# A planned start stage: finer steps, columns in other banks, and more work inside the plan

## Chip, core and metric

One core of one Trainium2 chip runs the program. The metric is device time in microseconds from launch to end; the kernel's inputs lie in HBM at the start and its output must lie there at the end.

## What is computed

Three layers, one behind the other: block-causal attention, a feed-forward layer with a maximum over three products, and a layer with eight experts of which each token takes two.

```python
def _attn_ref(q, k, v):                  # (4, 8, 576, 64) each
    scores = scale * np.matmul(q, k.transpose(0, 1, 3, 2))
    mask = block_i >= block_j            # blocks of 64 positions
    scores = np.where(mask, scores, -1000000000.0)
    ...                                  # softmax over the last axis
    return np.matmul(attn, v)

def _moe_ref(x, w1, w2, w3, w_out):      # x: (2304, 512), d_ff = 768
    h = np.maximum(np.maximum(x @ w1, x @ w2), x @ w3)
    return h @ w_out

def _moe2_ref(x, w_gate, w_noise, noise, w1, w2):
    noisy_logits = x @ w_gate + np.log1p(np.exp(x @ w_noise)) * noise
    ...                                  # top 2 of 8 experts, softmax over the two
    out[mask] += top2_w[mask, k, None] * (np.maximum(x[mask] @ w1[e], 0.0) @ w2[e])
```

Everything is fp32. Large products are made of three products of split operands (high and low part, fp32r); the first token unit and the early attention pairs use plain fp32 products, which the trace shows as two records each (0.43 us for 256 columns, from the hidden products).

## The kernel before

**Work.** Attention runs in 32 jobs, each a pair of heads of one batch; an "early" job (e) takes the first 256 queries, a "late" one (l) the other 320. The second layer runs in nine units of 256 tokens (`UT`). Unit 0 is computed in the start stage from early jobs 0 to 3 (batch 0), unit 2 from jobs 4 to 7 (batch 1). Behind the start stage a loop over jobs 8 to 31 sets steps of a job's attention beside steps of the units that are ready (`filler`, `gap`; one hidden step counts as 2.6 us in the code's own costs). Then the experts run one after the other.

**Start stage.** `start` (L598) lists steps with an engine, a cost, dependencies and a bank kind; `Plan.run` (L63) plays them through a list schedule and emits them in the order of their planned times, under `tc.manual_schedule()`, so each engine runs its steps in that order. A ready step with the longest chain behind it goes first (`level`). Where TensorE has no ready step before the first hidden product, a warming product on a spare bank is put in (`idle`, L603; `warm`, L132).

The steps: `first_load` brings queries (as two diagonal blocks, so that one product of 128 rows serves both heads; the rest of the tile is zeroed by `new_set`, L198), keys and values of jobs 0 to 3 over the SP and ACT queues. A job then goes through `e_scores` (L313, two steps h = 0, 1 of two blocks each), `e_max` on DVE, `e_exp` on ACT, `e_sums`, `e_scale` (on DVE for jobs 1, 2, 3, else on ACT), `e_turn` (transposes), `e_copy`, `e_values` (L429) and `e_out`. The weights w1, w2, w3 and w_out arrive as the 64-bit words of double floats, in 24 pieces (`load_piece`, twelve buffers); a piece is turned into fp32 by `integers` on DVE, `low_bits` on ACT and `join` on POOL. `first_hidden` (L554) computes the 18 half steps of unit 0's hidden layer, `first_max` the maxima, `first_columns` (L573) the product with w_out and with w_out times the gates (`gate_turn`, `gate_copy`, `gate_product`, `gate_out`, three groups). `split` makes the high and low halves of the weights for the other units (ACT and POOL). Banks: two "s", four "t"; the column products take a "t" bank.

**Behind the plan**, in program order but free for the scheduler to move, even ahead of the plan's end: `init_route`, `init_ids`, unit 0's route, the loads of job 8 (`load_scores`, `load_rest`) and of the first late job 9 (`load_job`, `load_values`), zeroing for it (`late_tiles`, L218), its split into halves (`prep_job`, L260), and job 8's scores. The loop over jobs 8 to 31 follows; while job 8 is transposed, job 9's five score blocks run (`s_block`).

## Time and profile before

| | us |
|---|---|
| median of three timed runs | 999.83 |
| lowest, highest | 998.15, 1004.65 |
| the profiled execution | 998.79 |
| its span, first to last instruction | 997.0 |

The profile page gives busy time by engine and in 40 slices of some 25 us; the granted clock is that of TensorE, in tenths of 2.4 GHz. Timelines list instructions in order of time, equal neighbours merged. A number in brackets behind a row is idle time of the engine just before it, and what ended it.

### The profile page before, as it was taken

The page shows a single profiled execution, that of the slowest core. Times are in us where ns is not written, and L with a number is a line of the kernel's source. Part 1 is how long each engine was busy: PE and PEld are TensorE (multiplying, and loading weights), DVE is VectorE, ACT ScalarE, POOL GpSimd, SP SyncE. Part 2 cuts the span into 40 slices and gives each one's busy share as a digit, 9 for nine tenths or more (in the row PEclk, how much of TensorE's full clock was granted, in tenths as well). Part 3 has the DMA queues.
Part 4 walks back from the last instruction along what each step waited for, and adds up shares of the span by engine and source line. Part 5 has one row for each costly group of instructions (what it writes and reads, how often), then busy time and mean ns, then how long its engine had stood idle before and what let it go on. Part 6 is the DMA issues. An engine that isn't in the chain of part 4 may idle for free. (4 is left out here: it accounts for less than half of the span.)

```text
span 997.0 us, 17056 instructions
## 1 busy us (share of the span) xinstructions
PE 975.0 (98%) x6558; PEld 872.7 (88%) x6558; DVE 429.1 (43%) x1260; ACT 396.8 (40%) x934; POOL 393.1 (39%) x303
## 2 busy tenths in 40 slices
PE   8979998999999999999999999999999999999997
PEld 5867897999999899899999899898898979898895
DVE  7872556664667566733157332221322222221321
ACT  6686345654545545541124143232322414132210
POOL 2875120130302213111320478664746556574302
PEclk9998999999999999999999999999999999999999
DMA  8931216121112111203013366553444344342101
GB/s 260 318 109 53 100 44 203 52 59 59 33 49 70 55 54 53 83 25 99 11 37 135 115 191 188 167 189 95 142 136 155 134 140 156 117 160 84 60 12 58
DMA packets 75860, 106.15 MB, mean 106 GB/s; under 512 B 23548, under 2 KB 48124, under 8 KB 75776
## 3 DMA queue, kind: packets, MB, share of 16 engines
q1 hardware_dynamic: 63408, 75.97, 24.5%
q0 software_dynamic: 10192, 28.28, 8.7%
q8 instruction: 52, 0.85, 0.4%
q10 hardware_dynamic: 2176, 0.79, 0.3%
q14 instruction: 32, 0.26, 0.1%
HBM read 85.35 MB, written 20.53 MB: 106 GB/s over the span
## 5 line engine op out<-in xcount | busy, mean ns | idle before, releaser
L173 POOL TENSOR_TENSOR w<-rw,w 128x1536 fp32r<-128x1536 f32 (+1 forms) x42 | 131.7, 3138 | 70.6 <-ACT w L172 55.1
L752 POOL TENSOR_TENSOR hl<-hm,hh 128x512 fp32r<-128x512 f32 x21 | 27.3, 1302 | 174.8 <-ACT hh L751 174.6
L172 ACT ACTIVATE w<-rw 128x1536 fp32r<-128x1536 f32 (+1 forms) x42 | 56.5, 1345 | 86.6 <-issue 42.1
L1108 PE MATMUL b<-xh,w 128*128 128x384 f32 (+7 forms) x272 | 87.3, 322 | 0.3 <-DVE xB L1113 0.3
L1110 PE MATMUL b<-xh,w 128*128 128x384 f32 (+7 forms) x272 | 87.6, 322 | 0.0
L1109 PE MATMUL b<-xl,w 128*128 128x384 f32 (+7 forms) x272 | 87.4, 321 | 0.0
L736 PE MATMUL t<-xA,w 128*128 128x256 f32 x288 | 82.8, 287 | 0.0
L737 PE MATMUL t<-xA,w 128*128 128x256 f32 x288 | 81.8, 284 | 0.0
L738 PE MATMUL t<-xA,w 128*128 128x256 f32 x288 | 81.5, 283 | 0.0
L265 POOL TENSOR_TENSOR Kl<-rk,Kh 128x576 fp32r<-128x576 f32 x16 | 23.0, 1436 | 122.6 <-ACT Kh L264 122.6
L1113 DVE SCALAR_TENSOR_TENSOR ht<-b,ht 128x384 fp32r<-128x384 f32 (+6 forms) x56 | 29.1, 520 | 94.5 <-ACT ht L1112 94.5
L1164 POOL DMA_INDIRECT out_rows<-y,isc x37 | 37.4, 1011 | 78.1 <-DVE y L1161 73.9
L1109 PE MATMUL t<-xl,w 128*128 128x256 f32 x240 | 67.3, 281 | 0.0
L1110 PE MATMUL t<-xh,w 128*128 128x256 f32 x240 | 67.3, 280 | 0.0
L1108 PE MATMUL t<-xh,w 128*128 128x256 f32 x240 | 67.3, 281 | 0.0
L1156 PE MATMUL b<-w,ht 128*128 128x512 f32 (+1 forms) x168 | 67.0, 399 | 0.0
L1158 PE MATMUL b<-w,ht 128*128 128x512 f32 (+1 forms) x168 | 66.4, 395 | 0.0
L1157 PE MATMUL b<-w,ht 128*128 128x512 f32 (+1 forms) x168 | 66.3, 394 | 0.0
L925 POOL DMA_INDIRECT ids<-rows,slots x36 | 35.7, 991 | 72.5 <-DVE slots L922 64.3
L736 PE MATMUL t<-xB,w 128*128 128x256 f32 x216 | 61.8, 286 | 0.0
L737 PE MATMUL t<-xB,w 128*128 128x256 f32 x216 | 61.2, 283 | 0.0
L738 PE MATMUL t<-xB,w 128*128 128x256 f32 x216 | 61.1, 283 | 0.0
(396 smaller groups left out, 2784.2 us busy)
## 6 DMA issues: line engine op xcount, KB each, us to landing
rw<-in_e SPq DMA_DIRECT2D x32, 768.0 KB, 4.6
w<-in_w SPq DMA_DIRECT2D x18, 512.0 KB, 8.0
rw<-in_e SPq DMA_DIRECT2D x16, 512.0 KB, 3.7
rk<-in_kT SPq DMA_DIRECT2D x16, 288.0 KB, 3.1
x2d<-x SPq DMA_DIRECT2D x18, 256.0 KB, 2.0
out_rows<-x SPq DMA_DIRECT2D x9, 512.0 KB, 3.1
w<-in_w_out SPq DMA_DIRECT2D x6, 512.0 KB, 7.6
rq<-in_qT SPq DMA_DIRECT2D x16, 160.0 KB, 2.6
```

The lines of the kernel that those rows point to most:

```text
L172: nc.scalar.activation(t[:, 0, :c], r[:, :c], AF.Copy)
L173: nc.gpsimd.tensor_sub(t[:, 1, :c], r[:, :c], plain(t[:, 0, :c]))
L736: nc.tensor.matmul(ps[:, j], wh, x[:, 0], start=kt == 0, stop=False)
L737: nc.tensor.matmul(ps[:, j], wh, x[:, 1], start=False, stop=False)
L738: nc.tensor.matmul(ps[:, j], wl, x[:, 0], start=False, stop=kt == 3)
L1108: nc.tensor.matmul(p, wt1(e, 0, kt, f), th[:, kt, c0:c1], start=kt == 0, stop=False)
L1109: nc.tensor.matmul(p, wt1(e, 0, kt, f), tl[:, kt, c0:c1], start=False, stop=False)
L1110: nc.tensor.matmul(p, wt1(e, 1, kt, f), th[:, kt, c0:c1], start=False, stop=kt == 3)
L1156: nc.tensor.matmul(ps, a, wt2(e, 0, f), start=f == 0, stop=False)
L1157: nc.tensor.matmul(ps, a, wt2(e, 1, f), start=False, stop=False)
L1158: nc.tensor.matmul(ps, l, wt2(e, 0, f), start=False, stop=f == 7)
L1164: st = nc.gpsimd.indirect_dma_start(out=out, out_offset=bass.IndirectOffsetOnAxis(ap=at, axis=0), in_=y, in_offset=None, bounds_check=NTOK ...
```

## The change

`Plan` gets ranks (lower goes first; `level` only breaks ties), a shared transfer model (`load`), banks that come free in the order in which they were taken, and no delay between steps of one engine. Costs are changed throughout. Queries of jobs 0 to 7 are loaded in one transfer as they lie, and `e_scores` makes two products of 64 rows (one per head, each to its half of the partitions) out of one of 128; job 8 and later ones keep the diagonal form. Column products become single steps and go to the bank that served as DVE's scratch (`shifted`) and to that of the warming products; gate and logit products take the gates as the stationary operand (16 columns) and stream 256 columns, and are copied and transposed back. Warming products may be put in until the second tile's first column product. The late pair's loads, zeroing and split, job 8's loads, scores and scaling and the noise load become steps of the plan; `init_route` and `init_ids` stand ahead of it, and a scheduling barrier without a semaphore behind it, so nothing that follows is moved ahead of the plan's end. The two row stores move behind the barrier, and one `gap(8)` more is put ahead of the loop. The core of the diff:

```diff
-
...
+    def add(self, engine, cost, emit, deps=(), rank=0.0, take=None, give=None, late=0.2, load=0.0):
...
+        def can(i, t):
+            x = self.ops[i][4]
+            if x and len(taken[x]) >= self.banks[x] and given.get(taken[x][-self.banks[x]], 1e9) > t:
+                return False
+            return all((own if self.ops[d][0] == self.ops[i][0] else done).get(d, 1e9) <= t for d in self.ops[i][3])
+
         while wait:
...
+                    taken[take].append(i)
...
-                t = min([x for x in [*free.values(), *done.values(), *(g[0] for g in gives)] if x > t])
+                t = min([x for x in [*free.values(), *done.values(), *given.values()] if x > t])
         for _, emit in out:
             emit()
         return max(done.values())
...
     def new_set(q, kv, p, pt):
-        q = q.rearrange("p (i c) -> p i c", c=128)
-        for r in range(2):
-            nc.gpsimd.memset(q[64 * r:64 * r + 64, :, 64 - 64 * r:128 - 64 * r], 0.0)
...
+    def late_queries(n):
+        QQ.append(att.tile([128, 5, 128], F32R, name=("Qh", "Ql")[n]))
+        nc.gpsimd.memset(plain(QQ[n]), 0.0)
+
+    def late_tails():
         for i in (4, 6, 8):
             nc.gpsimd.memset(PL[i][:, 64 * i + 64:], 0.0)
+
+    def clear_diagonal():
+        for r in range(2):
+            nc.gpsimd.memset(diagonal(SET[0][0])[64 * r:64 * r + 64, :, 64 - 64 * r:128 - 64 * r], 0.0)
...
+    def load_queries(j, eng):
+        eng.dma_start(early_set(j)[0][:, :256], qT[at(j):at(j) + 2, :, :256].rearrange("h d n -> (h d) n"))
+
+    def load_keys(j, eng):
+        eng.dma_start(early_set(j)[1], kT[at(j):at(j) + 2, :, :256].rearrange("h d n -> (h d) n"))
...
+        q = diagonal(SET[0][0])
         for r in range(2):
             nc.sync.dma_start(q[64 * r:64 * r + 64, :, 64 * r:64 * r + 64],
-                              qT[i + r, :, 0:256].rearrange("d (n c) -> d n c", c=64))
-        nc.sync.dma_start(k, kT[i:i + 2, :, :256].rearrange("h d n -> (h d) n"))
-
...
+        load_keys(j, nc.sync)
+
...
+            n = 64 * i + 64
+            if j >= 8:
+                nc.tensor.matmul(ps[:, x:x + n], diagonal(q)[:, i], k[:, :n], start=True, stop=True)
+                continue
+            for m in (slice(0, 64), slice(64, 128)):
+                nc.tensor.matmul(ps[m, x:x + n], q[m, 64 * i:64 * i + 64], k[m, :n], start=True, stop=True)
...
-    def gate_product(g):
-        ps = GS[g] = bank()
+    def gate_product(g, k):
+        ps = GS[g] = GS[g] if k else bank()
+        nc.tensor.matmul(ps[:2 * E, :256], GT[:, k], PL[7 + k // 2][:, 256 * (k % 2):256 * (k % 2) + 256],
+                         start=k == 0, stop=k == 3)
...
+    def logit_rows(key):
+        nc.scalar.activation(PL[6][:2 * E, :256], GS[key][:2 * E, :256], AF.Copy)
+
+    def logit_turn(key):
+        ps = GS[key] = bank()
         for j in range(2):
-            for k in range(4):
-                o = 256 * (k % 2) + 128 * j
-                nc.tensor.matmul(ps[:, 2 * E * j:2 * E * j + 2 * E], PL[7 + k // 2][:, o:o + 128], GT[:, k],
-                                 start=k == 0, stop=k == 3)
-
...
-    def first_columns(tt, w, n):
-        ps = C0["p"] = bank()
-        for ft in range(6):
-            nc.tensor.matmul(ps[:, :n], M0[ft // 2][:, ft % 2, tt * 128:tt * 128 + 128], w[ft], start=ft == 0,
-                             stop=ft == 5)
+    def first_columns(tt, ft):
+        if ft == 0:
+            C0["p", tt] = spare_bank if tt else shifted.bitcast(F32)
+        nc.tensor.matmul(C0["p", tt], M0[ft // 2][:, ft % 2, tt * 128:tt * 128 + 128], WPO[ft], start=ft == 0, stop=ft == 5)
...
+        def conv(n, rank):
+            LD[n] = add("SP", 0.45, lambda: load_piece(n), [AD[n - NW]] if n >= NW else [], rank, late=2.0, load=1.3)
...
+        def work(n, rank):
+            a = add("DVE", 1.45, lambda: integers(n), [LD[n]], rank, late=0.05)
+            b = add("ACT", 0.56, lambda: low_bits(n), [LD[n]], rank)
+            AD[n] = add("POOL", 1.0, lambda: join(n), [a, b], rank, late=0.1)
...
-            p = 30.0 + 0.1 * j
             if old is None:
-                LQ[j] = add("SP", 1.25, lambda: first_load(j, nc.sync, 0), [], 0.1 * j, late=2.0)
-                LV[j] = add("ACT", 1.25, lambda: first_load(j, nc.scalar, 1), [], 0.1 * j, late=2.0)
+                one, two = (nc.sync, nc.scalar) if j % 2 == 0 else (nc.scalar, nc.sync)
+                a, b = ("SP", "ACT") if j % 2 == 0 else ("ACT", "SP")
+                LQ[j] = [add(a, 0.65, lambda: load_queries(j, one), late=2.0, load=0.4),
+                         add(b, 0.65, lambda: load_keys(j, two), late=2.0, load=0.4)]
+                LV[j] = add(a, 0.65, lambda: load_rest(j, one), late=2.0, load=0.5)
                 return
-            LQ[j] = add("SP", 1.9, lambda: load_scores(j), [ES[old, 1]], p, late=2.0)
-            LV[j] = add("SP", 0.65, lambda: load_rest(j), [EV[old]], p, late=2.0)
+            LQ[j] = [add("SP", 0.45, lambda: load_queries(j, nc.sync), [ES[old, 1]], 1.0, late=2.0, load=0.4),
+                     add("SP", 0.45, lambda: load_keys(j, nc.sync), [ES[old, 1]], 1.0, late=2.0, load=0.4)]
+            LV[j] = add("SP", 0.45, lambda: load_rest(j), [EV[old]], 1.0, late=2.0, load=0.5)
...
             sb = "t" if j in (1, 3) else "s"
+            k = 2.5 if j > 3 else 0.0
...
-                s = ES[j, h] = add("PE", (0.76, 0.34)[h], lambda h=h: e_scores(j, h, sb), [LQ[j], LV[j]], p, take=sb)
-                m = add("DVE", (0.7, 0.45)[h], lambda h=h: e_max(j, h), [s], p)
-                ex.append(add("ACT", (0.9, 0.7)[h], lambda h=h: e_exp(j, h), [m] + ([ET[old]] if old is not None else []),
-                              p, give=None if h else sb))
-            r = add("DVE", 0.2, lambda: e_sums(j), ex, p, give=sb)
...
             sc = "DVE" if j in (1, 2, 3) else "ACT"
-            c = add(sc, 1.1 if sc == "DVE" else 1.35, lambda: e_scale(j, sc), [r], p)
+            c = add(sc, 1.3, lambda: e_scale(j, sc), [r], k, late=0.15)
...
+            if j < 4:
+                EX[j] = add("ACT", 0.3, lambda: e_out(j), [v], k, give=v)
+            else:
+                x = add("ACT", 0.35, lambda: e_out(j, 0), [v], k)
+                EX[j] = add("DVE", 0.4, lambda: e_out(j, 1), [x], k, give=v)
...
-                a = add("PE", 1.73, lambda fp=fp, m=m: first_hidden(fp, m, 0), d + hid[-1:], 100.0, take="t")
-                b = add("PE", 1.73, lambda fp=fp, m=m: first_hidden(fp, m, 1), [a], 99.0)
+                a = add("PE", 1.73, lambda fp=fp, m=m: first_hidden(fp, m, 0), d + hid[-1:], 1.0, take="t")
+                b = add("PE", 1.73, lambda fp=fp, m=m: first_hidden(fp, m, 1), [a], 1.0)
                 hid.append(b)
...
-            a = add("ACT", 0.41 * cost, lambda: split(n, i, j, src, False), deps, prio)
...
+        def part(n, i, j, src, deps, cost):
+            a = add("ACT", 0.41 * cost, lambda: split(n, i, j, src, False), deps, 4.0)
+            return add("POOL", cost, lambda: split(n, i, j, src, True), [a], 4.0, late=0.1)
...
-            done_g = add("PE", 1.7, lambda g=g: gate_product(g), cs + [gt], 60.0, take="t")
...
+            a = p = add("PE", 0.43, lambda g=g: gate_product(g, 0), cs[:1] + [gt], 2.5, take="t")
+            for k in (1, 2, 3):
+                p = add("PE", 0.43, lambda g=g, k=k: gate_product(g, k), [p, cs[k // 2]], 2.5)
+            b = add("ACT", 0.33, lambda g=g: logit_rows(g), [p], 0.5, give=a)
+            c = add("PE", 0.22, lambda g=g: logit_turn(g), [b], 0.5, take="t")
+            done_g = add("DVE", 0.15, lambda g=g: logit_out(g, WPG[:, 2 * g:2 * g + 2]), [c], 0.5, give=c, late=0.1)
...
-            a = add("PE", 5.2, lambda tt=tt: first_columns(tt, WPO, DM), [last, prev] + [AD[n] for n in range(18, 24)], 100.0, take="t")
-            last = add("ACT", 0.75, lambda tt=tt: first_out(tt), [a], 24.0, give="t")
-            add("SP", 0.7, lambda tt=tt: store(0, tt, C0[tt]), [last], 24.0)
-            a = add("PE", 1.3, lambda tt=tt: first_columns(tt, [WPG[:, ft] for ft in range(6)], 2 * E), [last] + go, 100.0, take="t")
-            last = add("DVE", 0.2, lambda tt=tt: first_gates(tt), [a], 24.0, give="t")
...
+            for ft in range(6):
+                p = add("PE", 0.86, lambda tt=tt, ft=ft: first_columns(tt, ft),
+                        [prev, *(AD[n] for n in (range(24) if ft == 0 else ()))] + ([p] if ft else []), 4.0)
+                if ft == 0:
+                    until = p
+            add("ACT", 0.46, lambda tt=tt: first_out(tt), [p], 0.5)
...
+        z = add("POOL", 0.66, clear_diagonal, [ES[7, 0], ES[7, 1]], 2.5)
+        q8 = add("SP", 2.1, lambda: load_scores(8), [z], 2.5, late=2.0, load=0.8)
+        x = add("SP", 0.9, lambda: load_job(first), [LD[23], gt], 3.0, late=2.0, load=1.5)
+        add("SP", 1.0, lambda: nc.sync.dma_start(noise_sb, noise.rearrange("(t p) e -> p t e", p=128)), [x, q8], 5.0, late=2.0, load=5.0)
+        v8 = add("SP", 0.45, lambda: load_rest(8), [EV[7]], 4.0, late=2.0, load=0.5)
+        add("SP", 0.45, lambda: load_values(first), [EV[6]], 4.0, late=2.0, load=0.8)
+        add("POOL", 0.45, late_tails, [], 4.0)
+        late_q = [add("POOL", 0.65, lambda n=n: late_queries(n), [ES[4 + n, 0], ES[4 + n, 1]], 3.0) for n in (0, 1)]
+        a = add("ACT", 0.68, lambda: split_keys(first, False), [x, EV[4]], 3.0)
+        add("POOL", 1.4, lambda: split_keys(first, True), [a, EV[5]], 3.0)
+        for r in (0, 1):
+            a = add("ACT", 0.47, lambda r=r: split_queries(first, r, False), [x, late_q[0]], 3.0)
+            add("DVE", 0.5, lambda r=r: split_queries(first, r, True), [a, late_q[1]], 3.0)
+        ex = []
+        for h in (0, 1):
+            a = add("PE", (0.76, 0.44)[h], lambda h=h: e_scores(8, h), [q8], 2.5, take="s")
+            b = add("DVE", (0.94, 0.67)[h], lambda h=h: e_max(8, h), [a], 2.5, late=0.15)
+            ex.append(add("ACT", (0.86, 0.64)[h], lambda h=h: e_exp(8, h), [b, ET[7]], 2.5, give=None if h else a, late=0.1))
+        b = add("DVE", 0.29, lambda: e_sums(8), ex, 2.5, give=a, late=0.1)
+        add("ACT", 1.3, lambda: e_scale(8, "ACT"), [b], 2.5)
+        return pl, idle, until
...
-        nc.sync.dma_start(noise_sb, noise.rearrange("(t p) e -> p t e", p=128))
...
-        nc.sync.dma_start(ids.rearrange("(p c) t -> p c t", p=128), z)
+        nc.gpsimd.dma_start(ids.rearrange("(p c) t -> p c t", p=128), z)
...
+    init_route()
+    init_ids()
     pl, idle, first_product = start()
     with tc.manual_schedule():
         pl.run(idle, first_product)
+    tc.no_sync_barrier()
     ph0.close()
+    for tt in range(2):
+        store(0, tt, C0[tt])
...
-    init_route()
-    init_ids()
...
-    load_scores(EJ[0])
-    load_rest(EJ[0])
-    late_tiles()
-    load_job(first)
-    load_values(first)
-    prep_job(first)
+    RAW.pop(first)
     load_job(late_after(first))
     load_values(late_after(first))
-    for f in score_steps(8):
-        f()
     scored(8)
+    gap(8)
```

## Rows read from the trace of the kernel before

**Rows 1.** Page, parts 1 and 2: PE over the span; granted clock in 40 slices.
```profile
PE 975.0 (98%) x6558; PEld 872.7 (88%) x6558; DVE 429.1 (43%) x1260; ACT 396.8 (40%) x934; POOL 393.1 (39%) x303
...
PEclk9998999999999999999999999999999999999999
```

**Rows 2.** Busy time by stretch: length; busy and count per engine; clock; DMA share; GB/s.
```profile
0.00:26.04 26.04, 22.49 (x129) 13.53 (x129) 18.94 (x71) 16.20 (x54) 7.43 (x26) 1.00 0.86 260
26.04:45.95 19.91, 19.37 (x90) 16.66 (x89) 18.64 (x28) 13.02 (x22) 15.68 (x16) 1.00 0.97 315
45.95:68.78 22.83, 20.54 (x114) 17.87 (x115) 16.66 (x43) 16.28 (x49) 20.43 (x20) 1.00 0.45 160
68.78:86.30 17.52, 14.33 (x100) 12.13 (x99) 7.27 (x24) 15.77 (x49) 5.20 (x4) 0.81 0.32 83
86.30:108.24 21.94, 20.94 (x84) 12.98 (x83) 5.25 (x15) 8.29 (x20) 13.02 (x12) 0.84 0.08 28
108.24:400.00 291.76, 287.42 (x2291) 264.54 (x2291) 180.11 (x590) 153.94 (x413) 58.34 (x48) 1.00 0.24 70
400.00:997.00 597.00, 589.95 (x3761) 534.96 (x3756) 182.27 (x496) 173.32 (x330) 272.98 (x181) 1.00 0.35 112
```

**Rows 3.** Waits of PE behind 108 us: total, times, longest.
```profile
PE t L426 <- ACT xB L455: 2.5, 1, 2.5
```

**Rows 4.** Busy time by stretch of the warming products (L135) alone.
```profile
0.00:26.04 26.04, 11.10 (x40) 4.08 (x40) 1.00 0.86 260
```

**Rows 5.** Timeline of ACT and its queue, start stage: start, duration, engine, line, operation.
```profile
1.51 0.62 ACTq L594 DMA_DIRECT2D kve<-in_v  x1
...
7.59 1.28 ACT L653 ACT_TABLE_LOAD   x1 [7.59 <-DMA Kl<-in_v]
8.88 0.47 ACT L329 ACTIVATE pe<-s,st 128x256 f32<-128x256 f32 x1
```

**Rows 6.** Timeline of SP's queue.
```profile
15.31 8.53 SPq L251 DMA_DIRECT2D rq<-in_qT  x1
```

**Rows 7.** Timeline of PE, 0 to 86 us (fp32 products show two records each).
```profile
5.13 1.44 PE L317 MATMUL s<-kve,qe 128*128 128x256 f32 x8 [0.70 <-POOL p L223]
...
46.98 1.89 PE L559 MATMUL t<-hl,w 128*128 128x256 f32 x8
48.71 0.92 PE L317 MATMUL s<-Kh,Qh 128*128 128x256 f32 x4
49.47 1.89 PE L559 MATMUL t<-hl,w 128*128 128x256 f32 x8
...
63.78 0.61 PE L317 MATMUL s<-Kl,Ql 128*128 128x64 f32 x4
64.22 1.86 PE L533 MATMUL t<-p,p 128*128 128x16 f32 x16
```

**Rows 8.** Timeline of PE, 81 to 105 us: values, score block, columns.
```profile
81.37 0.82 PE L426 MATMUL t<-Pl,V 128*64 128x256 f32 x8
82.02 0.82 PE L426 MATMUL t<-pte,kve 128*64 128x256 f32 x8
...
84.58 0.39 PE L277 MATMUL s<-Kh,Qh 128*128 128x320 f32 x1
...
86.30 4.45 PE L576 MATMUL t<-xB,hh 128*128 128x512 f32 x10
...
97.74 7.17 PE L576 MATMUL t<-xB,hh 128*128 128x512 f32 x10
```

**Rows 9.** Waits of POOL, 40 to 108 us.
```profile
POOL Kl L265 <- ACT Kh L264: 11.1, 1, 11.1
```

**Rows 10.** Groups by line, 0 to 108 us: busy, mean ns of one; idle before.
```profile
L500 DVE TENSOR_SCALAR sh<-w 128x512 int32<-128x512 int32 x24 | 16.7, 694 | 2.9 <-DMA w<-in_w 1.2 <-DMA w<-in_w_out 1.2
...
L548 POOL TENSOR_TENSOR w<-w 128x512 fp32r<-128x512 f32 x18 | 22.8, 1290 | 1.2 <-ACT w L550 1.2
```

**Rows 11.** Timeline of POOL: the first weight split.
```profile
43.28 1.28 POOL L548 TENSOR_TENSOR w<-w 128x512 fp32r<-128x512 f32 x1
```

## What I expected, before the run

> **What bounds the kernel now.** I read the page's first two parts first: TensorE is busy for 98% of the span, and the only slices with missing work or a low clock lie in the first ninth [rows 1]. The busy time by stage says the same in numbers. From 108.24 us, where the second token unit's products begin, to the end, PE is busy 877.4 of 888.8 us at a granted clock of 1.00, and the longest wait in there is 2.5 us [rows 2, 3]. That part is bound by PE itself: the change adds no product to it, so whatever it saves or costs ahead of 108.24 us moves the end by as much. The start stage is thus all that matters, and the reader should see three stretches in it.
>
> From 0 to 26.04 us early pairs 0 to 3 go through softmax before the first hidden product can start. PE is busy, but 11.1 us of it are warming products that compute nothing [rows 4]. From 26.04 to 45.95 us it is dense, PE 19.37 of 19.91. From 45.95 to 108.24 us PE is busy 55.81 of 62.29 us, and the granted clock is 0.81 and 0.84 in the last two stretches [rows 2].
>
> What was lost from 26.04 to 108.24 us: idle is 82.20 - 75.18 = 7.0 us, warming 0.5. For the clock: a mean of 0.81 over 17.52 us means 38% of it at 1.2 GHz, which loses half of 6.7 us, 3.3 us; 0.84 over 21.94 us loses 3.5. The second is to be seen directly: ten column products take 4.45 us at full clock and 7.17 us at the lower one [rows 8]. Sum lost: 14.3 us.
>
> No other engine fills the stage. From 0 to 108.24 us DVE is busy 66.8 us, ACT 69.6, POOL 61.8 (sums over five rows of [rows 2]). They wait for each other and for an order: POOL sits 11.1 us for one ACT copy (Kh) that stands behind ACT's other work, while part of its 24 weight splits of 1.29 us is still to do [rows 9, 10].
>
> **The change part by part.** *Loads of pairs 0 to 3.* Three transfers per pair instead of four, so six issues on each of SP and ACT instead of eight, and no zeroing of the diagonal before them. ACT now issues until its table load at 7.59 us, and its first exponential comes at 8.88 [rows 5]. The second issue starts at 1.51 and takes 0.62 us [rows 5]; six end near 4.6, with 1.28 us of table 5.9, so exponentials could start near 5.9: 3.0 us earlier. The first scores, now at 5.13 us [rows 7], must be there by then: the keys of pair 0 are now the first issue on their queue and not the second, so they land some 0.6 us earlier, and with 0.9 us of maximum behind a first score step at 4.5 us this holds.
>
> *Order of pairs 0 to 3.* They get rank 0, so the integers and low bits of the weights no longer stand ahead of a ready step. From the first exponential to the first hidden product it takes 17.2 us now. DVE is busy 18.94 us until 26.04 [rows 2]; five pieces of 1.4 us in it [rows 10] and some 1.5 us of setup are not of this chain, which leaves it some 10.5 us of DVE. Bounds of this edit: 0 (a step that has begun still delays) and 3.5 us gained; I take 1.5, since pieces still slip into gaps. Together the first hidden product goes from 26.04 to 21.5 us: **-4.5 us**, bounds 0 and -6.5.
>
> *Supply of the hidden products.* A half step takes 1.73 us (46.98 to 48.71 [rows 7]); two of them need two weight pieces, each twice 0.694 us of DVE [rows 10], with gaps some 1.45, plus 0.4 us of maxima: 3.3 us against 3.46. So DVE follows, barely. The noise load (2304 pieces of 32 bytes) goes behind everything; now the load behind it holds SP for 8.53 us [rows 6], in which no weight piece is issued. Taking that away costs nothing and keeps the pieces ahead of DVE. Who waits for noise is unit 0's route, behind the plan, and no product.
>
> *Columns in spare banks, single products.* The column products (24 records of 0.43 us, 10.3 us) leave the four rotating banks and may run as soon as the hidden maxima and the weight pieces exist; with the lowest rank on PE they fill the gaps of pairs 4 to 7 instead of standing at 86.30 and 97.74 us [rows 8]. Gate products become four of 256 columns instead of sixteen of 16: the sixteen show 1.86 us, eight records of 256 columns, as many as the four make, 1.89 [rows 7]. Each of four groups gets a small transpose and an ACT copy, some 0.2 us of PE each: +0.9 us. Warming products now fill every gap of the plan until the second tile's columns, so the clock should stay at 2.4 GHz.
>
> *Early scores in halves.* One block-diagonal product of 128 rows becomes two of 64 rows, to the two halves of the partitions of one bank. One pair's two steps take 0.76 and 0.44 us now (48.71 to 49.47, 63.78 to 64.22 [rows 7]). No row shows a 64-row product. The nearest are the value products, which already write two halves of 64 partitions: eight records (four products, 768 columns, which at a half step's 0.43 us for 256 would make 1.3 us one after the other) take 0.65 us (81.37 to 82.02 [rows 8]), so halves run side by side. Bounds: 0 if these do too, and +1.1 us a pair if not, 4.4 for pairs 4 to 7, whose scores lie in the dense part, and about 1 more in the chain of the first four. I take 0, by the nearest row.
>
> Here a rule speaks against the change. The Trainium skill (TensorEngine Tiling (Array Packing), Restrictions and Gotchas) has it that different row tiles cannot access one PSUM bank at the same time. The halves are row tiles into one bank, unlike the value products, which are column tiles with all 128 rows; no run here shows yet whether it holds for different partitions of a bank. By it the sum would have the upper bound above.
>
> *Moved in:* the late pair's loads, split and zeroing and pair 8's loads, scores and scaling were already done before 108 us; as planned steps they only get a place (Kh on ACT no longer late for POOL). Taken as 0. One wait is new on SP: pair 8's query load waits for POOL to zero the diagonal after pair 7's scores, and the late pair's, noise and value loads stand behind it; PE needs none of them before the plan ends. *Moved out:* pair 9's score blocks (84.58 to 86.30 [rows 8] and 1.2 us more) and pair 8's turn, 0.6, 3.5 us in all. They come behind a scheduling barrier and PE works on them there as long as here: 0. The row stores, the second late pair's loads and unit 0's route start behind the plan; nothing on PE waits for them. The slot table's store goes to POOL's queue at the start, where POOL is busy 7.4 of 26 us [rows 2].
>
> *How much of the 14.3 us comes back?* All engines have room. But pairs 4 to 7 still wait for DVE until the integers are done, and ACT has most of the splits, four scalings and the gate copies left then. From 45.95 to 68.78 us, where steps of all kinds are mixed, 2.3 of 22.83 us are idle [rows 2]; over some 35 us behind the hidden products I estimate 4 us by that. So 14.3 - 4 - 0.9 = **-9.4 us**, bounds -4 and -13.4.
>
> **Sum.** -4.5 - 9.4 = -13.9 us. The profiled execution took 998.8 us (span 997.0): 984.9. The median of the runs shown is 1 us above the profiled one, which lies within their own spread of 6 us, so 985.
>
> **Rivals.** (A) The sum above, 985, own range 979 to 993. (B) The halves of the scores run one after the other: +4.4 and +1, 990. For it speaks that no 64-row product is in the trace; against it the value products. (C) ACT and POOL take over: splits get the lowest rank, and unit 2's third group needs 14 of them, 14 x 1.29 = 18 us of POOL. In the trace the first comes at 43.28 us [rows 11], but now every other ready step goes first; if it slips to 88, that group waits until 106, two groups (5 us) behind unit 2's start, so a start at 101 against 104.7 now on the same footing (108.24 less the 3.5 moved out): gain 4, 995. Against it: ACT's busy sum leaves it 38 of 108 us free. (D) Slower: the warming products are put where the plan expects a gap; where the chip's waits fall elsewhere they come on top. With the 6.5 us of idle of 45.95 to 108.24 us filled so, none of the waits gone and no earlier start, 998.8 + 6.5 = 1005. It decides when the plan's gaps add up to more than its order saves. Against it: from 26 to 46 us, where the present plan holds little but hidden products, it runs without a gap.
>
> **How the numbers follow.** A 0.60, B 0.12, C 0.16, D 0.12. A change of less than 1% is about what a measurement of this kernel can't tell from none: bounds 989.8 and 1009.8. Faster: nearly all of A and half of B, 0.62. Slower: half of D, with other losses on top, 0.06. Same: the rest, 0.32. The range reaches from 2 us below A's best to C and part of D: 977 to 1001.
>
> **What would show it.** First hidden product near 21.5 us and the hidden ones dense to about 53; score steps of pairs 4 to 7 at 0.76 and 0.44 us (B: 1.5 and 0.8); granted clock 1.00 to the end of the stage; columns broken up among pairs 4 to 7; unit 2's first product near 90 us. C would show as PE waiting for a POOL split at the stage's end, D as many warming products behind 26 us with the same waits beside them. I would be wrong altogether if the part behind 108 us grew, for instance because pair 9's chain now starts cold.

## The result, and the profile after it

The changed kernel takes 988.56 us (median of four runs, 985.66 to 993.39) against 1001.74 for the kernel before beside it: a ratio of 0.9875, interval 0.9847 to 0.9904. The profiled execution went from 998.79 to 985.66 us, 13.1 us less; the sum said 13.9 less.

The page of the changed kernel, parts 1 and 2, answers [rows 1]: TensorE's share of the span goes from 98% to 99%, and no slice has a lower clock any more.

```profile
PE 970.9 (99%) x6594; PEld 861.5 (88%) x6594; DVE 430.2 (44%) x1259; ACT 395.9 (40%) x938; POOL 392.0 (40%) x298
...
PEclk9999999999999999999999999999999999999999
```

Busy time by stretch, with the columns of [rows 2]: to the first hidden product, to the last, to unit 2's first product, and on to the end.

```profile
0.00:22.07 22.07, 20.86 (x157) 11.87 (x157) 16.37 (x60) 16.01 (x55) 5.40 (x18) 1.00 0.92 323
22.07:53.15 31.08, 31.08 (x146) 27.32 (x144) 27.96 (x43) 18.96 (x32) 21.08 (x20) 1.00 0.84 296
53.15:90.60 37.45, 37.45 (x226) 19.73 (x224) 15.64 (x54) 32.44 (x100) 28.81 (x28) 1.00 0.12 23
...
108.24:400.00 291.76, 287.68 (x2285) 263.57 (x2284) 180.21 (x570) 155.70 (x423) 57.87 (x48) 1.00 0.24 70
400.00:983.90 583.90, 576.87 (x3656) 522.91 (x3655) 173.81 (x474) 166.09 (x312) 271.92 (x180) 1.00 0.35 112
```

From 22.07 to 90.60 us PE is busy in all of 68.53 us at a clock of 1.00; 1.6 us of that are five short warming products. Before, 82.20 us lay between the same two marks [rows 2].

Timeline of PE, with the columns of [rows 7]. L149 is a warming product, L358 a score step in halves, L608 a hidden product of unit 0, L625 a column product, L811 the first product of unit 2.

```profile
1.08 4.02 PE L149 MATMUL wm<-ones 128*128 128x512 bf16 x9 [1.08 <-DVE ones L143]
5.03 1.13 PE L358 MATMUL s<-kve,qe 64*64 64x256 f32 x8
6.00 0.92 PE L358 MATMUL t<-Kh,Qh 64*64 64x256 f32 x8
6.75 0.92 PE L358 MATMUL s<-Kl,Ql 64*64 64x256 f32 x8
...
22.07 31.24 PE L608 MATMUL t<-hl,w 128*128 128x256 f32 x144
...
61.47 1.13 PE L625 MATMUL sh<-xB,hh 128*128 128x512 f32 x2
...
89.43 1.02 PE L625 MATMUL wm<-hl,hh 128*128 128x512 f32 x2
90.38 0.29 PE L582 MATMUL t<-ident,p 16*128 16x16 f32 x2
90.60 0.38 PE L811 MATMUL t<-xA,w 128*128 128x256 f32 x1
```

All 18 half steps of the hidden layer stand in one row: nothing came between them in this execution (e0 below shows how little room there is). The column products are twelve rows from 61.47 to 89.43 us instead of the two blocks of [rows 8].

Waits of PE behind unit 2's start, as [rows 3]. `cum` is the running count of tokens per expert that a unit's route keeps:

```profile
PE s L313 <- DVE gl L845: 1.9, 1, 1.9
PE t L467 <- ACT Pl L416: 1.1, 2, 0.9
PE s L313 <- DVE cum L964: 0.7, 1, 0.7
PE s L355 <- ACT Ph L416: 0.7, 1, 0.7
```

**Where the 13.1 us came from.** Unit 2's first product moved from 104.7 us (108.24 less the 3.5 us of work moved behind it) to 90.60: 14.1 us. Of these 4.0 lie ahead of the first hidden product and 10.2 behind it. Behind unit 2's start 893.3 us remain (983.9 - 90.60) where 892.3 were left before (997.0 - 104.7): 1.0 us is given back.

### The profile page after: what moved, and what is told of

Its sections match the earlier page's. It is cut to its first block, busy times and chain, and to the rows that moved or that the text cites. A ratio compares the mean times of both kernels' runs of the same rounds, so it can differ in the third digit from the quotient of the medians.

```text
span 983.9 us, 17138 instructions
## 1 busy us (share of the span) xinstructions
PE 970.9 (99%) x6594; PEld 861.5 (88%) x6594; DVE 430.2 (44%) x1259; ACT 395.9 (40%) x938; POOL 392.0 (40%) x298
## 5 line engine op out<-in xcount | busy, mean ns | idle before, releaser
L811 PE MATMUL t<-xA,w 128*128 128x256 f32 x288 | 82.8, 287 | 0.0
L811 PE MATMUL t<-xB,w 128*128 128x256 f32 x216 | 61.8, 286 | 0.0
## 6 DMA issues: line engine op xcount, KB each, us to landing
w<-in_w_out SPq DMA_DIRECT2D x6, 512.0 KB, 10.2
```

The source lines that it names most:

```text
L811: nc.tensor.matmul(ps[:, j], wh, x[:, 0], start=kt == 0, stop=False)
```

## Experiments

Each is the changed kernel with one edit; e1, e8 and e11 have a line or two more, which give out tiles in whatever order the plan asks for them. "Behind" is the span less the start of unit 2's first product. Each time is a median, the ratio is to the kernel before on the same chip (medians 999.9 to 1001.7 us), in brackets its 95% interval. "Last split" is where POOL's last weight split ends, counted from unit 2's start. The last three columns come from the profiled execution, which can lie up to 3 us from the median (changed kernel 985.66, e9 1001.27). The intervals of e1, e2, e5, e6, e8 and e11 overlap e0's. All runs of e1, e2, e5 and e8 are above all of e0's (at most 989.36), those of e6 (from 987.51) and e11 (from 989.17) are not.

| run | us | ratio | unit 2 from | behind | last split |
|---|---|---|---|---|---|
| changed kernel | 988.56 | 0.9875 [0.9847, 0.9904] | 90.60 | 893.3 | +4.9 |
| e0 the same again | 987.05 | 0.9872 [0.9833, 0.9910] | 91.90 | 893.7 | +4.9 |
| e7 10 us more | 997.48 | 0.9967 [0.9952, 0.9982] | 100.63 | 896.1 | -5.0 |
| e1 diagonal | 993.97 | 0.9927 [0.9899, 0.9955] | 100.78 | 893.2 | +4.9 |
| e10 halves, old transfers | 995.25 | 0.9947 [0.9924, 0.9971] | 99.18 | 893.2 | +4.9 |
| e5 noise early | 990.80 | 0.9904 [0.9870, 0.9938] | 93.01 | 894.6 | +4.9 |
| e6 unplanned | 990.20 | 0.9900 [0.9859, 0.9941] | 94.19 | 892.5 | +3.2 |
| e4 no ranks | 999.69 | 1.0002 [0.9985, 1.0019] | 106.06 | 891.3 | -12.3 |
| e2 columns last | 991.75 | 0.9905 [0.9867, 0.9943] | 99.95 | 890.3 | -7.0 |
| e8 columns grouped | 990.87 | 0.9913 [0.9883, 0.9943] | 93.08 | 897.5 | +2.9 |
| e3 warming until hidden | 994.50 | 0.9944 [0.9925, 0.9964] | 91.84 | 901.2 | +8.9 |
| e9 first scores sooner | 999.00 | 0.9984 [0.9967, 1.0001] | 90.41 | 909.0 | +9.7 |
| e11 e9, splits sooner | 989.94 | 0.9886 [0.9865, 0.9907] | 90.98 | 898.5 | -2.9 |

**e0 and e7: does the end follow the stage?** e0 is the changed kernel unedited. e7 puts 46 warming products at the plan's end:

```diff
+        add("PE", 9.94, lambda: warm(bank(), 46), [c], 6.0)
```

> The changed kernel once more, as the measure for the runs beside it. Theory A (the start stage alone moved): ratio to the kernel before 0.987, first unit-2 product near 90.6 us. The rival, that the first comparison caught a lucky execution, would give 0.995 or more.

> 46 products of 512 columns (9.9 us at full clock) that compute nothing are added on PE at the end of the plan. A: behind the plan the kernel is bound by PE, so the end moves by as much, +9 to +10 us on the changed kernel. Rival: something else (weights split on POOL, DVE's work on unit 0's route) bounds the next stretch, and part of it is hidden: +5 us or less.

e0 repeats the result within 1.5 us. Its hidden products are not quite dense, though: they wait 0.8 us for a weight piece that POOL has to join.

```profile
48.19 6.31 PE L608 MATMUL t<-hl,w 128*128 128x256 f32 x28 [0.83 <-POOL w L557]
```

e7 costs 10.4 us against e0 and 8.9 against the first timing, for products of 9.9 us: the part behind is bound by PE, as the first view said, and time in the stage moves the end by about as much. It is not exact: what is left behind unit 2's start varies with the order there, from 890.3 in e2 to 896.1 in e7, and up to 909.0 in e9 (below).

**e1 and e10: are halves free?** e1 goes back to products of 128 rows, which needs the queries as two diagonal transfers (pieces of 256 bytes) and zeroing; e10 keeps those transfers and the products in halves.

```diff
-        eng.dma_start(early_set(j)[0][:, :256], qT[at(j):at(j) + 2, :, :256].rearrange("h d n -> (h d) n"))
+        q = diagonal(early_set(j)[0])
+        for r in range(2):
+            eng.dma_start(q[64 * r:64 * r + 64, :, 64 * r:64 * r + 64],
+                          qT[at(j) + r, :, 0:256].rearrange("d (n c) -> d n c", c=64))
```

> Undoes one part: the early scores of pairs 0 to 7 are one product of 128 rows again, with two diagonal query transfers a pair and the zeroing ahead of them; the rest of the plan stays. A: 64-row halves run side by side, so the products cost the same (0.75 against 0.76 us for the large step); only the head feels the two extra issues and the zeroing, first hidden product 1 to 1.5 us later, total +1 to +2 us on the changed kernel. Rival: the halves carry a good part of the gain, +4 us or more.

> 64-row products as in the changed kernel, but the queries of pairs 0 to 7 come in two diagonal transfers a pair of 256-byte pieces again (no zeroing, since the products read only the blocks). It parts the run with the diagonal products, 7 us slower, into product and transfer. New theory A: the transfers make it; on SP the reloads of pairs 4 to 7 stand ahead of weight pieces 12 to 17 and hold them back, so the hidden products stall some 6 us for a join on POOL at the last third, and the total is 5 to 7 us above the changed kernel's 987. Rival: the products (and the zeroing) make it, 0 to +2 us.

e1 lost 6.9 us against e0 where 1 to 2 were expected, so that was a miss; e10 lost 8.2 with the halves kept, so the loss is the transfers'. SP's queue, first in e1, then in the changed kernel (weight pieces have the tile `w`, queries of pairs 4 to 7 are Qh, Ql and the like), with e1's wait of PE:

```profile
24.73 4.03 SPq L260 DMA_DIRECT2D Qh<-in_qT  x2
...
35.82 3.52 SPq L543 DMA_DIRECT2D w<-in_w  x5
```
```profile
21.86 0.33 SPq L256 DMA_DIRECT2D Qh<-in_qT  x1
...
29.48 2.48 SPq L538 DMA_DIRECT2D w<-in_w  x5
```
```profile
PE t L613 <- POOL w L562: 6.4, 2, 6.1
```

The queries and keys of pairs 4 to 7 (the reloads of the tiles of pairs 0 to 3) stand ahead of weight pieces 12 to 17 on SP. As diagonals they take longer (4.03 us is the longest of the four). The pieces are issued 6.3 us later, of which 2.3 were lost before the reloads began (18.43 us against 16.12), and the hidden products wait 6.4 us for a joined piece. In e1 the first hidden product is 2.2 us later than in e0 as well; in e10 it is 0.3. In e10 the wait is 5.0 us, and it costs again through the clock: from 52.72 to 57.00 us behind it the granted clock reads 0.50, and the last 28 records take 9.33 us where e0's take 6.31. The products alone are no longer in doubt: a step in halves goes from 6.00 to 6.75 us in the changed kernel, 0.75 us, against 0.76 for 128 rows [rows 7]. The Trainium skill (TensorEngine Tiling (Array Packing), Restrictions and Gotchas) rules out two row tiles in one PSUM bank at a time; for halves that go to different partitions of the bank, no row here bears that out.

**e5 and e6: noise and the moved-in work.** e5 issues the noise load behind weight piece 8. e6 takes pair 8's steps and the late pair's out of the plan, and the barrier and the one `gap(8)` more away, so that these steps follow the plan as before the change.

```diff
+                if n == 8:
+                    nc.sync.dma_start(noise_sb, noise.rearrange("(t p) e -> p t e", p=128))
```
```diff
-    tc.no_sync_barrier()
...
+    clear_diagonal()
+    load_scores(8)
...
+    prep_job(first)
```

> The noise load (2304 pieces of 32 bytes) stands on SP right behind weight piece 8, as before the change, unknown to the plan. By the prediction, which took its move at nothing, the pieces stay ahead of DVE: hidden products dense, 0 to +1 us. Rival, after the run with the diagonal products: the supply behind the head is tight, pieces 12 to 17 come some 5 to 8 us late and the hidden products stall for that, total +4 to +7 us.

> The late pair's loads, zeroing and split and pair 8's loads, scores and scaling are no steps of the plan (they stay in it as empty steps, so the order of the rest is the same), stand behind it as before and may be moved ahead by the scheduler; no barrier. A, as predicted: being planned is worth nothing by itself, -1 to +2 us. Rival: planning them is a main part of the gain, because moved steps get in the plan's way on ACT and SP, +5 us or more.

e5 costs 3.7 us by the medians and 2.0 between the profiled executions: the three pieces behind the noise hold SP from 12.78 for 9.96 us, and PE waits 2.7 us for a joined piece at 49.30, where e0 waits 0.8. Lying between the two expectations, and with e0's wait beside it, it says that the supply has next to no room. e6 costs 3.1 us by the medians, 1.1 between the profiled executions, and its runs mix with e0's, so whether it costs anything is not shown. PE waits 1.3 us for a joined piece; the late pair's three loads now stand ahead of the pieces on SP. Its unit 2 starts at 94.19, but with some 2 us of pair 8's turn and pair 9's score blocks ahead of it, as before the change, so its start and its 892.5 behind are not on the others' footing.

**e4, e2, e8: order and columns.** e4 drops the ranks; e2 lets columns wait for pairs 4 to 7; e8 makes each tile's six column products one step.

```diff
-                i = max(ready, key=lambda i: (-self.rank[i], level[i], -i))
+                i = max(ready, key=lambda i: (level[i], -i))
```
```diff
-  [prev, *(AD[n] for n in (range(24) if ft == 0 else ()))] + ([p] if ft else []), 4.0)
+  [prev, *(AD[n] for n in (range(24) if ft == 0 else ()))] + [EX[j] for j in range(4, 8)] + ([p] if ft else []), 4.0)
```
```diff
+            p = until = add("PE", 5.16, lambda tt=tt: [first_columns(tt, ft) for ft in range(6)], ...
```

> The ranks are not used, the longest chain behind a step decides alone; steps, banks, costs and transfers stay. A: weight pieces step in between the softmax of pairs 0 to 3 again, first hidden product 1.5 to 3 us later, and the gap filling behind the hidden products is in part lost; +3 to +6 us. Rival: the finer steps and true costs suffice, 0 to +1.5 us.

> The column products stay single and in the spare banks, but the first of each tile also waits for the outputs of pairs 4 to 7, so they can't fill gaps. A: 20 of the 24 column records lie before the last value product now, 8.6 us; taken from there their place is filled with warming products and they follow at the end, so unit 2 starts 7 to 9 us later (near 98 to 99 us) and the total grows by as much. Rival: ranks, costs and the earlier head make the gain; at most +2 us.

> The changed kernel with the six column products of each tile as one planned step of 5.16 us again, in the same spare banks. Theory (the gain behind 53 us is from the columns being off the rotating banks and free in time, their size matters little): 0 to +3 us, 987 to 991; each of the two groups delays a ready step of pairs 4 to 7 by up to 5 us, part of which other work fills. Rival (single products are what fills the gaps): first product of unit 2 at 95 or later and +4 us or more, 992.

e4 loses 12.6 us against e0, the whole gain, where 3 to 6 were expected. Not in the head: its first hidden product comes at 22.14 us. The hidden products break off after ten half steps for a gap that the plan itself sees and fills with warming products:

```profile
40.74 14.42 PE L149 MATMUL wm<-ones 128*128 128x512 bf16 x66
```

The weight pieces are not late there: POOL has joined the fifteenth at 40.09 us, at 41.86 in the changed kernel. But DVE turns all 24 pieces before anything else, and its first maximum of the hidden products (L618) comes at 57.39 us instead of 29.25. In the plan that maximum gives back the bank for the sixth hidden product, which would explain the gap behind the fifth (ten half steps); it was not tried by itself. So what the ranks buy is DVE's order: the maxima between the pieces. e2 moves unit 2 by 8.0 us against e0 but the end by 4.7 only, because less is left behind. e8 costs 3.8 us by the medians; of the 5.0 between the profiled executions 1.2 are unit 2's start and 3.8 lie behind it. The size of the column steps matters little for the stage itself.

**e3, e9, e11: what lies behind unit 2's start.** e3 allows warming products only until the first hidden product. e9 corrects the plan's costs of the first loads, so three warming products fewer stand ahead of the first scores. e11 is e9 with ACT's halves of the weight splits at rank 2.5.

```diff
-        return pl, idle, until
+        return pl, idle, hid[0]
```
```diff
-                LQ[j] = [add(a, 0.65, lambda: load_queries(j, one), late=2.0, load=0.4),
-                         add(b, 0.65, lambda: load_keys(j, two), late=2.0, load=0.4)]
+                LQ[j] = [add(a, 0.45, lambda: load_queries(j, one), late=1.0, load=0.4),
+                         add(b, 0.45, lambda: load_keys(j, two), late=1.0, load=0.4)]
```
```diff
-            a = add("ACT", 0.41 * cost, lambda: split(n, i, j, src, False), deps, 4.0)
+            a = add("ACT", 0.41 * cost, lambda: split(n, i, j, src, False), deps, 2.5)
```

> The changed kernel, but warming products may be put in only until the first hidden product, so the five short ones behind 53 us go. Theory (clock stays at 1.00 because the broken-up columns fill the gaps, not because of warming): granted clock 1.00 in 53 to 90.6 us, time 987 to 989, no change against the changed kernel (988.6 and 987.1 in its two timings). Rival (the few warming products hold the clock up): clock near 0.9 in that stretch and +3 us, 991. Second rival (warming products delay ready work): -1.5 us, the sum of the five.

> The changed kernel, with the plan's cost of the first loads of queries and keys at 0.45 and 1.0 us in place of 0.65 and 2.0. The data of pair 0 land 2.9 us behind their issue at 0.76, but nine planned warming products hold PE until 5.03 us. Theory (prediction's step 'first exponential at 5.9' missed by 1.4 us for these products): first scores near 4.0, first exponential near 6.3, first hidden product 21.0 instead of 22.1, 1 us less, 987. Rival (the chain of DVE and ACT through four pairs sets the first hidden product): first hidden unchanged at 22, 988.6 or 0.

> The kernel with the first scores sooner (999.0 us, unit 2 from 90.41 us, last weight split on POOL until 100.1, 909 us behind unit 2's start against 893 in the changed kernel), with one number more changed: ACT's halves of the weight splits get rank 2.5 in place of 4, so POOL gets them some 10 us sooner. Theory (splits that run on past unit 2's start slow DVE's small operations for unit 0's route, and unit 2's maxima on ACT and pair 9's on DVE stand behind the route): last split before 94 us, the small operations at 0.2 us again instead of 1.1 to 1.2, no PE wait over 2 us between 95 and 110 us, clock 1.00 there, unit 2 from 92 to 95, 890 to 893 us behind it: 984 to 989 us, 10 to 15 us less than with the first scores sooner. Rival (the end of the plan on PE decides, and ACT's halves now stand ahead of the chain of pairs 4 to 7): unit 2 3 us later with the same 909 behind it, 1002. Second rival (the loss there comes from the order that the scheduler gives the route, with splits early or late): 995 to 999.

e3 and e9 were both misses. In e3 the clock from 53 to 90 us stayed at 1.00 without the five products, as expected, and yet it cost 6 to 7 us. In e9 the first scores did start at 3.75 us instead of 5.03, but ran at half the rate (steps from 3.75 to 5.30 to 6.79 us), the first hidden product stayed at 21.97, as the rival had it, and 10 us were lost. Both lose behind unit 2's start. In e3 it is one wait and the clock behind it; first the wait, then the stretch (columns as [rows 2]):

```profile
PE s L313 <- DVE cum L964: 3.9, 1, 3.9
```
```profile
105.00:110.00 5.00, 3.71 (x17) 3.24 (x19) 4.47 (x20) 1.96 (x6) 0.00 (x0) 0.66 0.26 98
```

The profile names `cum`, a step of unit 0's route, because it ended last. What PE waits for is a score bank, which the reciprocal of pair 9's row sums (L395) frees, as the e9 rows name it; it stands on DVE between the route's steps. PE begins 0.14 us behind its end in e3, in e9 and in the changed kernel.

In e9 it is more. Waits of PE from 90 to 130 us, two stretches, and the instructions on POOL, DVE and ACT that lead to the first wait:

```profile
PE t L811 <- ACT hm L816: 3.8, 1, 3.8
PE s L355 <- ACT pe L390: 1.8, 1, 1.8
PE s L313 <- DVE st L395: 1.1, 1, 1.1
```
```profile
100.00:105.00 5.00, 1.95 (x9) 1.95 (x10) 4.68 (x29) 0.69 (x2) 0.14 (x1) 0.74 0.57 210
105.00:110.00 5.00, 3.93 (x16) 3.38 (x16) 3.92 (x10) 1.68 (x5) 0.00 (x0) 0.50 0.28 105
```
```profile
92.27 6.29 POOL L597 TENSOR_TENSOR w<-xB,w 128x512 fp32r<-128x512 f32 x5 [1.88 <-ACT w L599]
98.50 1.30 POOL L597 TENSOR_TENSOR w<-hl,w 128x512 fp32r<-128x512 f32 x1
...
89.96 0.19 DVE L586 COPY gl<-t 128x32 f32<-128x32 f32 x1 [5.14 <-PE t L582]
...
95.04 1.06 DVE L932 TENSOR_SCALAR rt<-rt 128x16 f32<-128x16 f32 x1 [4.54 <-ACT rt L931]
...
96.13 1.22 DVE L933 TENSOR_SCALAR rt<-rt 128x16 f32<-128x16 f32 x1
...
98.67 1.16 DVE L937 TENSOR_TENSOR rt<-rt 128x16 f32<-128x16 f32 x1
...
91.50 2.70 ACT L599 ACTIVATE w<-xB 128x512 fp32r<-128x512 f32 x5
...
94.81 0.20 ACT L931 ACTIVATE rt<-gl 128x16 f32<-128x16 f32 x1
...
102.31 0.21 ACT L970 ACTIVATE ex<-ex 128x2 f32<-128x2 f32 x1 [4.71 <-DVE ex L969]
102.42 0.58 ACT L816 ACTIVATE hm<-t 128x512 f32<-128x512 f32 x1
```

Read upwards: PE waits 3.8 us for a bank that ACT's copy of unit 2's first maximum (L816) empties. That copy stands behind L970 of unit 0's route, which waits for the route's small operations on DVE. Two things make these late. Four of them, on 16 columns, take 1.06 to 1.22 us each while POOL is still splitting weights, as long as a split (6.29 us for five). And they begin late: the logits (`gl`) are there at 90.15 us, but the route's first step on ACT (L931) stands behind seven of ACT's own halves of the splits (L599), and DVE waits 4.5 us for it. Behind PE's wait the granted clock reads 0.74 and 0.50.

The slow operations alone can't be the difference to the changed kernel, which has them too: from L962 to L939 its route loses 3.9 us to them against e11's times, e9's 4.3. But there L931 follows the logits (90.90 us) at once:

```profile
91.30 0.21 ACT L931 ACTIVATE rt<-gl 128x16 f32<-128x16 f32 x1
```

From the logits to L970 it is 8.0 us in the changed kernel and 12.2 in e9, and the delay of L931, 4.7 us against 0.4, makes up the 4.2 between them. In e3 L931 comes 4.9 us behind the logits.

e11 gets the splits done before unit 2 starts. The same two operations, then PE's longest wait from 90 to 130 us and the stretch in which it lies:

```profile
91.77 0.18 DVE L933 TENSOR_SCALAR rt<-rt 128x16 f32<-128x16 f32 x1
...
92.22 0.14 DVE L937 TENSOR_TENSOR rt<-rt 128x16 f32<-128x16 f32 x1
```
```profile
PE s L355 <- ACT pe L390: 1.8, 1, 1.8
```
```profile
115.00:120.00 5.00, 3.53 (x18) 2.37 (x20) 1.91 (x7) 2.23 (x6) 0.00 (x0) 0.81 0.18 43
```

0.18 and 0.14 us, no wait of PE of 2 us, clock 1.00 from 95 to 115 us, and 9.1 of e9's 10.4 us are back, with unit 2 0.6 us later. From the logits to L970 it is 5.4 us. Both rivals (1002; 995 to 999) are out. But the edit takes away both causes at once, since ACT's halves are through before L931 as well, so the expectation's theory of slow operations is not shown by it; the comparison with the changed kernel speaks for ACT's order as the larger part. Of the 890 to 893 us expected behind, though, 898.5 came: 5.2 more than in the changed kernel. Added up in stretches of 5 us from unit 2's start (PE's idle time, and the share of the clock below 1.00 times the stretch, without the idle tail), e11 has 13.2 + 3.4 us and the changed kernel 11.8 + 0. The difference of 4.8 accounts for nearly all; half of the 3.4 lies behind the 1.8 us wait for ACT's scaling of a later pair (L390) shown above. The same sum for e9 is 19.1 + 8.6, 15.9 more against 15.7 measured. In e11 ACT's L816 also stands ahead of L970 again; how much of e9's loss is this order, how much the late L931 and how much the slow operations was not separated. Nor do the splits explain the whole column "behind": e7 and e8 have 896 and 897 with earlier ones. The wait for L390 is what these share: 2.0 us in e7, 1.9 in e8, 1.8 in e9 and e11, against 0.7 at the same line (L355) in the changed kernel. In these four, ACT's copies of the late pair's transposes (L416), which wait for PE, stand ahead of L390; in the changed kernel they stand behind it. e2 has them ahead too and no such wait, so this alone does not make it, and it was not tried.

No experiment beat the changed kernel. Not tried by themselves are the new costs and the bank rule of `Plan`, the gate products as rows, and the barrier.

## Why the prediction came out right, point by point

**What bounds the kernel.** Right, by e7: 9.9 us in, 8.9 to 10.4 us out.

**Loads and first exponential: -3.0, measured -1.5.** The table load ends at 6.03 us, near the 5.9 worked out. But the exponential waits 1.31 us for the maxima:

```profile
4.33 0.39 ACTq L269 DMA_DIRECT2D V<-in_v  x1
4.75 1.28 ACT L699 ACT_TABLE_LOAD   x1 [4.75 <-DMA Qh<-in_qT]
7.34 0.47 ACT L370 ACTIVATE pe<-s,st 128x256 f32<-128x256 f32 x1 [1.31 <-DVE st L364]
```

The step "with 0.9 us of maximum behind a first score step at 4.5 us this holds" failed: the first scores came at 5.03, and from there it is 2.3 us to the exponential, 1.2 of them until DVE begins its maxima. The nine warming products ahead of the scores take 0.45 us each, the twenty at 10.75 us 0.22 (4.49 us): PE starts at half its rate. Fewer of them did not bring the first hidden product forward by more than executions differ: 21.97 us in e9 and 21.39 in e11, against 21.41 to 22.70 in the runs with this head unchanged.

**Order of pairs 0 to 3: -1.5, measured -2.5.** From the first exponential to the first hidden product it is 14.7 us, where 17.2 were read before; within the bound of 3.5. Both together: 22.07 us against 21.5 forecast. The head was thus right as a sum of two terms missed in opposite directions, which is luck.

**Supply: right on the products, too easy on its margin.** "Taking that away costs nothing and keeps the pieces ahead of DVE" understates it: with the noise back among the pieces (e5) some 2 to 4 us are lost, and in e0, with nothing changed, the hidden products wait 0.8 us for a join. The gap between 3.3 and 3.46 us per pair of half steps was there to warn of it.

**Halves: 0, right.** 0.75 us a step at the start. Two first steps among pairs 5 and 6 show 0.90, but a step of 128 rows in the same stretch (73.36 to 74.21 us) shows 0.85. Rival B is out.

**Stage: -9.4, measured -10.2.** Idle time is 0.0 where 4 us were left in the sum, warming 1.6. By that alone -9.4 should have become -11.8. Of the other 1.6 us, 0.7 were counted twice in the 14.3: of the 6.8 us for the clock, 0.7 lie between 72.0 and 73.8 us, where PE was idle and the 7.0 us of idle time hold them already. Another 0.5 are the columns, whose twelve steps take 10.8 us from start to start where 10.3 were counted. The rest is not settled. That the term came out within 1 us is luck too, since its parts missed by more. The gate transposes were counted with 0.9, the work moved out with 3.5 us; neither was tested.

**Moved in 0, moved out 0.** Moved in: e6 gives no clear price for leaving it out of the plan (1 to 3 us, its runs mixed with e0's). Moved out: the step "unit 0's route start behind the plan; nothing on PE waits for them" failed, though at most some 1 us came of it here. PE's 0.7 us at `cum` L964 above is the bank of pair 9 that waits among the route's steps on DVE. Timelines of POOL and DVE, first of before, then of the changed kernel:

```profile
101.05 0.39 POOL L548 TENSOR_TENSOR w<-xs,w 128x96 fp32r<-128x96 f32 x1
...
108.22 0.16 DVE L858 TENSOR_SCALAR rt<-rt 128x16 f32<-128x16 f32 x1
```

```profile
93.83 1.28 POOL L597 TENSOR_TENSOR w<-hl,w 128x512 fp32r<-128x512 f32 x1
95.06 0.39 POOL L597 TENSOR_TENSOR w<-xs,w 128x96 fp32r<-128x96 f32 x1
...
92.57 1.32 DVE L932 TENSOR_SCALAR rt<-rt 128x16 f32<-128x16 f32 x1
93.93 1.20 DVE L933 TENSOR_SCALAR rt<-rt 128x16 f32<-128x16 f32 x1
```

Before, the last split ended at 101.44 us, 6.8 ahead of unit 2's start, and the route's first operation took 0.16 us. The change brought unit 2 forward past the splits, which have the lowest rank, and the same operation takes 1.32. That is rival C's place, ACT and POOL behind with the splits, with another victim: not unit 2's own products but unit 0's route, on DVE by slow operations and, where ACT's halves are late as well, on ACT. With 4.9 us of splits past unit 2's start 1.0 us was given back; how much of it is the route's is not shown, for PE's idle time behind unit 2's start is 11.8 us against 11.4 before. With 8.9 (e3) it was 7.9 more, and with 9.7 (e9) 15.7 more in the profiled execution and 10.4 by the medians; in these two L931 came late. The forecast named "the part behind 108 us grew" as what would make it wrong, and a slightly different plan would have done so.

**Rival D** (warming on top) did not happen here, since the plan's gaps shrank to 1.6 us; e4 shows what it looks like, at 14.42 us.

## What to carry to other kernels

A term of 0 for work that is only moved deserves a range: look at what its engines share with what is still running at its new place, and at what stands ahead of its first step on each of them. When a stage gets shorter, check what had been finishing just ahead of its end; the lowest-ranked work is now past it. A planned order should be judged by the first 30 us behind the plan too, since changes of 1 us in it moved the total by 10.

## What the runs showed of the hardware

- Small DVE operations beside POOL's splits: TENSOR_SCALAR on 16 columns takes 1.20 to 1.32 us in the changed kernel and 0.17 to 0.18 in e11, where POOL is done. A RECIPROCAL at 98.51 us in e9, beside the last large split, took its usual 0.24. The Trainium skill (SBUF — State Buffer, Who interferes with whom) states a lock for the whole instruction on a port pair that both engines share, taken by some forms of DVE operation and not by others; these rows agree with it.
- Waits of some 2 to 5 us cost again through the clock: in e9 the first 40 us behind unit 2's start have 6.8 us of idle time and lose 5.2 more at the lower clock; in e10 the clock reads 0.50 for 4.3 us behind a wait of 5.0.
- Two products of 64 rows into different partitions of one bank run side by side: a score step of four such products takes 0.75 us, and 0.76 as two products of 128 rows.
- A transfer of the queries in pieces of 256 bytes on SP's queue held it 1.26 to 4.03 us for two issues (e1, pairs 4 to 7), where the one issue of long rows takes 0.33 to 0.69 in the changed kernel and once 1.28 in e0.
